# Chunk 1's first matrix product in a retention-plus-MLP kernel: seven block products for eight, and a new order table

## The chip, the cores and the metric

The kernel runs on one core of one Trainium2 chip. The metric is the device time of one execution in microseconds (us); smaller is better.

## What is computed

A retention layer (a linear attention with a decaying state, 4 batches, 8 heads, 768 steps, head size 64) feeds an MLP with a tanh-gelu:

```python
gamma = 1.0 - 2.0 ** (-5.0 - np.arange(H))
for t in range(S):                                   # S = 768
    state = gamma * state + k[:, :, t] (outer) v[:, :, t]
    y[:, :, t] = scale * q[:, :, t] @ state
x = y.transpose(0, 2, 1, 3).reshape(B * S, H * D)    # 3072 x 512
h = x @ w_in                                         # 512 x 2048
g = gelu_tanh(h)
out = g @ w_out                                      # 2048 x 512
```

## The kernel before

**Chunks.** The 768 steps are cut into six chunks of 128 steps; all four batches of a chunk make 512 tokens. For each chunk `att(c)` computes the retention output x (transposed, in fp16): it loads q, k and v, casts or scales them, transposes them on TensorE (`mm_T2`, L283, 64x64 matmuls against the identity), forms the scores (`mm_A`, L294), masks them on VectorE (L345), adds the part from the carried state (`mm_yc`, L313) and the part from the chunk itself (`mm_yi`, L325), and updates the state (`mm_s`, L336). Then M1 is h = x @ w_in with the gelu, and M2 is g @ w_out.

**Two forms of M1.** With plain blocks M1 takes 128 matmuls of 128x256 for a chunk. `m1_raw(c)` does that in 16 bank-fills of 8 matmuls each (`moe1_mm`, L426); each fill is read by one gelu on ScalarE (L442). `m1_w(c)` uses a Strassen-like scheme (`PROD`): both operands are seen as 2x2 blocks, and four groups `g` each do seven products of four matmuls (`m1w_mm`, L549), 112 in all. It pays with side work: sums of w_in blocks (`u_w`, made once on VectorE, L451), four sums of x blocks per chunk (`xs`, on GpSimd, L451; numbers 1 and 3 need all of x, 2 needs 1, 4 needs 2), and for each group three copies of a partial result from PSUM to SBUF (kind `snap`, L220, on ScalarE), three adds (kind `add`, L451, on VectorE) and four gelus, of which three read SBUF. Before the change chunk 0 uses `m1_first` (plain, as its x arrives batch by batch), chunk 1 uses `m1_raw`, and chunks 2 to 5 use `m1_w`. M2 of chunk 0 is plain (`m2_mm`, L572); M2 of chunks 1 to 5 has seven products (`m2w_mm`, L561) with sums of g (`s_g`, `sumg` on VectorE or GpSimd).

**What sets the order.** After a hand-written prologue every piece of work is an item with a kind, a list of what it needs and what it gives. `ORDER` is a table written out in the kernel: each word is an engine letter (p TensorE, a ScalarE, v VectorE, g GpSimd, s SyncE) and an item number, and the items are emitted in that order, so it fixes the order of every engine's queue, and by it which buffer an item takes (the slot that came free first). A word w puts idle matmuls on TensorE. `KIND` lists the engines on which a kind may run. An engine works through its queue in order: an instruction that waits holds up all behind it.

**Loads.** SyncE issues the loads of q, k and v as one chain of items in a fixed order (`load_in`, L791; for chunks 3 to 5 q comes as sixteen small transfers, `q_load`, L734), and the output stores (L582) stand between them where the table puts them. The chain begins behind a small copy on GpSimd (`hold`, L780), which waits for the third part of w_out. The loaded tiles are cast from fp32 to fp16 on GpSimd or VectorE (L222) or on ScalarE (L220), or scaled (L237).

**The in-place sum.** Sum number 3 of w_in (`sumw`, j = 3) overwrites a block of w_in itself, so it has to wait until the last plain reader is done. Before, that is `m1_raw` of chunk 1, group by group (`("m1raw", 1, i)`).

Of the kernel before, what the change touches and what calls it, by code (L numbers as in the profile page):

```python
# [18 lines left out]
s13 v137 v140 s14 s15 s16 s17 s18 a178 s19 g29 s20 s21 g26 v164 v156 v24 v157 v25 v141 s22
s23 p193 g35 s36 s37 p189 p187 a186 v153 v27 v147 v28 p207 a206 p209 p223 p225 a224 g32 s38  # L20
p211 p195 p197 p227 a194 a210 a196 p229 p199 p213 a222 p231 s39 a192 s40 a208 v149 s41 a226
a212 a198 p233 a232 p215 a214 a188 p217 p219 a216 v165 a230 a228 p201 a200 p203 p205 a202
a204 p806 p807 p808 p809 p810 p235 p811 p812 p221 p237 a236 p813 a218 a220 p814 p815 a816
p240 v238 v239 p246 v244 p818 a245 p243 p249 a234 v247 v241 v242 p262 p821 p824 v139 v248
v33 p825 p265 v158 a822 p267 v30 v31 v151 v34 a264 p826 a266 p827 p277 a276 a819 s42 s43 s44
s45 s46 p279 g58 g59 a828 s47 p252 a278 v155 s48 s823 a250 p258 v257 v251 p281 a256 p283
p285 a280 a282 a284 p261 v143 s829 v260 v259 p255 p263 v253 v254 p287 p289 a288 p271 a286
v150 p275 v167 v270 p269 a268 p273 p291 p293 p295 p297 v159 p299 v166 a49 a52 p301 a53 a50
v274 a292 a294 v272 a290 v310 v138 g55 g56 p338 a296 p326 a298 v308 v312 p344 a300 v146 s817
a336 a343 a337 s61 s820 s62 s63 v313 p303 a302 p305 p307 g51 s64 v309 g60 v324 v325 v316  # L30
a342 p347 p332 s65 a304 v54 a306 g320 p329 g57 g317 a331 g318 g321 v327 g322 v346 v345 v328
p830 p831 s66 a330 p335 v334 p341 v339 v340 v333 a832 p833 p834 v835 s67 p349 a74 p348 p357
p351 v350 p359 p361 v356 p355 g78 p353 v352 p836 p837 v154 p383 a384 p400 a401 p366 a367
v311 v358 v354 g362 g364 a70 a76 a72 p402 v314 g82 g363 p385 p839 s68 p840 s69 a838 v360
v403 v315 v386 a387 p368 v369 p373 g84 s86 s87 p388 p371 a372 a374 a389 a404 p417 p390 p842
v71 a418 a391 g365 g323 g77 g73 a370 p375 p843 s88 s89 v79 p405 p378 g80 v142 s90 v376 a377
p381 p395 p392 v319 v379 v83 a841 p419 v396 a380 p845 a406 a397 a382 g434 g435 g81 v420 v75
p407 p422 a408 a423 p409 g85 v162 v393 a394 v410 p424 a425 p412 v413 p426 v844 p398 p415
v427 a411 a416 p429 v430 a421 a399 p846 v847 s848 p452 v450 s91 p461 a414 a459 p432 a433
v460 p853 v451 v438 a431 g439 a428 g446 g447 g440 a99 g101 v442 g443 p467 p458 v465 p455  # L40
v453 v454 v456 g449 p849 v457 p850 a851 s852 s92 s93 v466 p854 p464 p469 v462 p468 p473 v463
p471 p479 a95 p481 a97 v470 v472 p477 v476 a107 p475 p856 v474 g482 p857 s94 g484 a103 v478
v480 v98 v96 p520 s111 a521 g436 p486 p488 g445 g105 g483 a855 v858 g102 p522 p503 a504 a487
a109 s112 s113 s114 s115 g106 g448 v489 g441 g485 g437 p859 v523 g110 p525 a526 p527 a528
p860 s116 s117 a490 p491 p532 p508 a524 p505 a509 v533 a534 p862 v506 v104 v108 a507 v444
p493 a494 p512 p510 v100 a511 a492 v513 a861 p537 p863 a864 p515 v516 a538 p495 v496 p498
a517 v499 a500 p529 p542 p539 v540 p865 a497 p501 a502 p544 p518 a545 v530 a519 p535 p866
p868 v554 a514 a120 v558 g559 v867 p869 v870 p549 a543 a541 a122 a536 g555 g557 a531 g562
v550 p872 a551 p546 p581 s871 s118 a579 v547 p572 v580 v570 a571 v556 p873 a874 v563 s875
p552 a553 a548 g566 p575 v574 v573 p584 g568 p587 p876 p877 p879 g567 p880 a878 g564 v585  # L50
p578 v582 v586 g560 v583 v577 v576 p589 p588 p591 p597 p595 g123 p601 v590 v596 v594 p599
p593 v592 g602 v600 g561 g603 v598 p882 p883 s119 a128 a132 a134 p885 a124 p606 a607 p640
p625 p623 a641 v881 g604 a884 a624 v626 p886 a887 p608 v609 p888 p889 p613 a614 v121 p630
a631 p628 a629 p642 a627 v569 v129 v133 p611 a612 p618 g135 v643 a644 p635 a610 p645 v636
a637 v619 p632 v633 a620 p615 p657 a634 g130 a658 v616 g126 a646 g565 p891 p647 g131 g605
p664 a665 p621 p638 a648 a622 a617 v890 g127 p649 v650 a651 a639 g678 p892 v893 s894 v676
p652 v653 p662 p669 p659 a663 v660 v670 p895 p896 p666 a661 a671 a654 v674 p655 g675 a656
p899 v667 a668 p672 a673 p701 a699 p692 v682 a897 v680 v691 v679 s898 g683 v686 v690 a700
p900 v687 g689 p902 p903 p707 p704 p695 g684 a901 v904 p905 p906 p908 a907 p909 v702 a910
g688 v125 v694 p911 v705 p698 v693 v706 v703 g681 g685 p709 p708 p912 v697 v696 p715 p717  # L60
p711 p713 v677 v710 v712 p914 p915 p773 a774 v716 v714 v916 s917 p722 g718 g720 p724 a723
v725 p756 a757 p739 a740 p729 a730 g719 p758 v759 a726 p775 v776 p744 p727 a760 a728 a745
p741 v742 p778 p746 g721 a777 a747 p734 v735 p761 p731 p763 v732 p748 v749 a743 p780 v913
a736 a764 p751 v752 p737 p754 p768 a779 a781 p785 a733 v786 a738 g790 g791 a762 v769 a755
a753 a750 a787 a770 g794 p918 p765 v766 g795 p782 v783 a767 p922 a784 p771 a772 p788 v798
a789 v802 p924 v803 p919 v805 a920 p926 v799 p928 a923 p930 s921 v927 v800 a925 p932 a933
p934 p936 a931 v793 v797 a935 a937 v804 v801 v792 v796 p938 v929 v939 p940 p943 p946 p949
v944 v941 s942 p952 a945 a950 v947 a951 a953 s948 s954
"""


# [1 line left out]
def kernel(  # L73
# [10 lines left out]
    B, H, S, Dh = q.shape  # L84
    C = 128
# [355 lines left out]
    def gelu(out, in_):  # L441
        nc.scalar.activation(out=out, in_=in_, func=AF.Gelu_apprx_tanh, scale=1.0)  # L442
# [357 lines left out]
    def att(c):  # L800
# [125 lines left out]
                S1(b)  # L926
        for par in range(2) if 0 < c < NCk - 1 else ():
            S(par)
        for j in (1, 3, 2, 4) if c > 1 else ():
            def emit(eng, j=j):  # L930
                xs[c] = T["xs", c]
                sum_of(eng, j, RHS, x_of4(c))

            need = {1: [("x", c, b) for b in range(B)], 3: [("x", c, b) for b in range(B)],
                    2: [("xs", c, 1)], 4: [("xs", c, 2)]}[j]
            op("sumx", emit, need + ([] if j == 1 else [("al", "xs", c)]), [("xs", c, j)],
               alloc=[(("xs", c), 1)] if j == 1 else [], early=[("al", "xs", c)] if j == 1 else [])
# [9 lines left out]
    def m1_first():  # L947
        for t0, t1, bs, cost, kind in ((0, half, (0, 1), 0.873, "gelu"), (half, half + C, (2,), 0.45, "gelu2"),
                                       (half + C, 2 * half, (3,), 0.45, "gelu2")):
            for fp in range(NP):  # L950
# [13 lines left out]
                   alloc=[(("g", 0, fp // 2), 1)] if new else [], early=[al] if new else [],  # L964
                   free=[key])
                last = [("m1done", 0)] if fp == NP - 1 and t1 == 2 * half else []
                pe(cost, emit, [("x", 0, b) for b in bs] + [("win" if fp else "winh", fp // 2)] + after("M1", t0), [key] + last,
                   [(key, 1, (128, 2, half))], [("x", 0)])

    def m1_raw(c):  # L970
        for t in range(2):
            for fp in range(NP):
                key = ("bank", "h", c, fp, t)

                def emit(fp=fp, t=t, key=key):
                    for r in range(2):
                        moe1_mm(c, 2 * fp + r, T[key][:, r], t * half, t * half + half)

                def ev(eng, fp=fp, t=t, key=key):
                    g_sb[c, fp // 2] = T["g", c, fp // 2]  # L980
                    gelu(g_tile(c, 2 * fp)[:, :, t * half:(t + 1) * half], T[key])

                new = fp % 2 == 0 and t == 0
                al = ("al", "g", c, fp // 2)
                op("gelu", ev, [key] + ([] if new else [al]),
                   [("H", c, fp, i, t) for i in range(2)],
                   alloc=[(("g", c, fp // 2), 1)] if new else [], early=[al] if new else [],
                   free=[key])
                last = fp == NP - 1 and t == 1
                pe(0.873, emit, [("x", c, 2 * t), ("x", c, 2 * t + 1)] + [("win", fp // 2)] + after("M1", c),  # L990
                   [key] + ([("m1raw", c, fp // 2)] if t and fp % 2 else []) + ([("m1done", c)] if last else []),
                   [(key, 1, (128, 2, half))], [("x", c)] if last else [])
# [322 lines left out]
```

## Time and profile before

| | |
|---|---|
| median of the runs shown | 196.97 us (196.82 to 198.26, 3 runs) |
| the profiled execution, own time | 199.29 us |
| its span, first to last instruction | 197.5 us |
| granted TensorE clock | 1.000 |
| busy: TensorE / VectorE / ScalarE / GpSimd | 189.3 / 142.1 / 123.0 / 104.6 us |
| matmuls | 2793 |
| L426 (plain M1 matmuls) | 320, 29.8 us busy |
| L549 (M1 matmuls in seven products) | 448 (rows xs,u_w; xs,w_in; x,w_in; x,u_w) |
| instruction DMAs (queues 8 and 14) | 22 and 7 packets, 0.42 MB |

A line number is that of the kernel before; a helper such as L451 (`tt`) or L220 (`copy_on`) serves many items, so its groups are told apart by the names of the tiles. Busy time of TensorE counts overlapping matmuls once. Idle time is put down to what released the engine. L549 before is chunks 2 to 5; the plain matmuls of chunk 1 are 128 of the 320 of L426.

### The profile page before, as it was taken

How to read it: one execution, taken by the hardware profiler on the slowest of the kernel's cores; microseconds unless marked ns; L12 is line 12 of the kernel's file. 1: busy time of each engine (PE TensorE's matmuls, PEld its weight loads, DVE VectorE, ACT ScalarE, POOL GpSimd, SP SyncE). 2: the span in 40 equal slices, each digit the busy share in tenths (PEclk: the TensorE clock that was granted, in tenths of full speed). 3: DMA queues.
4: the chain of work that ended last, by engine and by line, in shares of the span. 5: the costliest groups of instructions: out<-in, count | busy, mean ns of one | idle time of the engine just before them, and what ended most of it. 6: DMA issues, size and time to landing. Idle time of an engine off the chain costs nothing.

```text
span 197.5 us, 6582 instructions
## 1 busy us (share of the span) xinstructions
PE 189.3 (96%) x2793; PEld 154.2 (78%) x2793; DVE 142.1 (72%) x284; ACT 123.0 (62%) x237; POOL 104.6 (53%) x112
## 2 busy tenths in 40 slices
PE   7799999999999799999999999999999999999993
PEld 2357995556887688788888888888888888888882
DVE  4375042888599799779999885888867697675930
ACT  3367681143778611999948989629598810799321
POOL 2678000020107681997699995698953490818000
PEclk9999999999999999999999999999999999999999
DMA  6999999999989756998899879902002110200205
GB/s 151 287 261 205 207 206 196 247 238 204 205 214 231 207 91 137 238 208 135 157 257 240 153 132 226 311 32 53 3 0 110 47 63 3 106 0 3 108 3 212
DMA packets 96285, 30.06 MB, mean 152 GB/s; under 512 B 88320, under 2 KB 93184, under 8 KB 96256
## 3 DMA queue, kind: packets, MB, share of 16 engines
q1 hardware_dynamic: 84976, 23.35, 50.4%
q0 software_dynamic: 4752, 4.19, 13.2%
q10 hardware_dynamic: 6528, 2.10, 4.2%
q8 instruction: 22, 0.36, 0.7%
q14 instruction: 7, 0.06, 0.1%
HBM read 27.54 MB, written 6.29 MB: 171 GB/s over the span
## 4 chain that ended last, share of the span: by engine, by line
PE 80%; DMA 7%; SPq 6%; ACT 2%; issue 1%; POOL 1%; ACTq 1%; DVE 0%
PE ps L561 28%; PE ps L549 24%; PE ps L426 13%; PE ps L572 7%; SPq L734 6%; DMA w_in<-in_moe_w_in_dram 3%; DMA st<-in_k_dram 3%; PE ps L294 3%; PE ps L325 2%; PE ps L283 2%; DMA ldq<-in_q_dram 1%; PE ps L336 1%; PE ps L313 1%; ACT qk L220 1%; POOL qk L237 1%
## 5 line engine op out<-in xcount | busy, mean ns | idle before, releaser
L451 DVE TENSOR_TENSOR st<-ps,st 128x512 f32<-128x512 f32 x48 | 31.5, 683 | 12.2 <-ACT st L220 6.4
L442 ACT ACTIVATE g<-ps 128x512 f16<-128x512 f32 (+1 forms) x56 | 28.6, 547 | 16.0 <-PE ps L426 14.9
L561 PEld LDWEIGHTS <-s_g 128*128 128x128 f16 x320 | 30.8, 98 | 4.2 <-issue 0.2
L345 DVE TENSOR_TENSOR a<-ps,mask 128x512 f16<-128x512 f32 x44 | 27.4, 682 | 6.7 <-PE ps L294 6.5
L220 ACT COPY st<-ps 128x512 f32<-128x512 f32 x48 | 26.3, 598 | 8.6 <-PE ps L549 8.5
L442 ACT ACTIVATE g<-st 128x512 f16<-128x512 f32 x48 | 29.1, 644 | 1.7 <-DVE st L451 1.5
L426 PE MATMUL ps<-x,w_in 128*128 128x256 f16 (+1 forms) x320 | 29.8, 252 | 0.3 <-DMA w_in<-in_moe_w_in_dram 0.3
L426 PEld LDWEIGHTS <-w_in 128*128 128x128 f16 x320 | 25.5, 98 | 3.6 <-DMA w_in<-in_moe_w_in_dram 0.5
L451 POOL TENSOR_TENSOR s_g<-g 128x512 f16<-128x512 f16 x18 | 21.3, 1192 | 12.5 <-ACT g L442 12.5
L549 PEld LDWEIGHTS <-w_in 128*128 128x128 f16 x256 | 24.9, 98 | 3.2 <-ACT st L220 0.3
L220 ACT COPY o<-ps 128x512 f32<-128x512 f32 (+1 forms) x28 | 14.3, 532 | 19.9 <-PE ps L561 15.9
L561 PEld LDWEIGHTS <-g 128*128 128x128 f16 x240 | 22.9, 98 | 3.1
L549 PEld LDWEIGHTS <-u_w 128*128 128x128 f16 x192 | 18.7, 98 | 2.9 <-DVE st L451 0.7
L561 PE MATMUL ps<-w_out,s_g 128*128 128x256 f16 x160 | 19.6, 273 | 0.0
L561 PE MATMUL ps<-w_out,g 128*128 128x256 f16 x160 | 19.3, 273 | 0.0
L220 ACT CAST qk<-ldq 64x512 f16<-64x512 f32 (+1 forms) x19 | 11.5, 623 | 12.6 <-DMA ldq<-in_q_dram 7.5
L561 PE MATMUL ps<-t_w,s_g 128*128 128x256 f16 x160 | 19.1, 273 | 0.0
L451 POOL TENSOR_TENSOR s_g<-s_g,g 128x512 f16<-128x512 f16 x13 | 15.1, 1168 | 6.4 <-DVE s_g L451 6.1
L549 PE MATMUL ps<-xs,u_w 128*128 128x256 f16 x128 | 17.8, 273 | 0.5 <-DVE st L451 0.5
L549 PE MATMUL ps<-xs,w_in 128*128 128x256 f16 x128 | 17.6, 273 | 0.0
L549 PE MATMUL ps<-x,w_in 128*128 128x256 f16 x128 | 16.6, 273 | 0.0
L237 POOL TENSOR_TENSOR v<-ld,cst 128x512 f16<-128x512 f32 x14 | 14.8, 1069 | 1.8 <-DMA ld<-in_v_dram 1.8
(74 smaller groups left out, 277.7 us busy)
## 6 DMA issues: line engine op xcount, KB each, us to landing
ld<-in_v_dram SPq DMA_DIRECT2D x19, 256.0 KB, 4.4
ld<-in_k_dram SPq DMA_DIRECT2D x17, 256.0 KB, 5.0
out_dram<-o SPq DMA_DIRECT2D x8, 512.0 KB, 3.4
ldq<-in_q_dram SPq DMA_DIRECT2D x48, 64.0 KB, 2.6
w_out<-in_moe_w_out_dram POOLq DMA_DIRECT2D x4, 512.0 KB, 14.2
w_in<-in_moe_w_in_dram POOLq DMA_DIRECT2D x3, 512.0 KB, 7.7
ld<-in_q_dram SPq DMA_DIRECT2D x5, 256.0 KB, 5.8
out_dram<-o SPq DMA_DIRECT2D x5, 256.0 KB, 4.3
```

The lines of the kernel that those rows point to most:

```text
L220: eng.copy(out=out, in_=in_)
L237: eng.tensor_tensor(out=o, in0=heads(src, sw), in1=heads(cst[:, col:col + H].unsqueeze(2), sw).broadcast_to([128, NHP, 2, Dh]), op=ALU.mult,)
L283: nc.tensor.transpose(out=ps[m][j * 64:(j + 1) * 64, n + i, hp], in_=h16[nm, c, b][rows, 2 * hp + j], identity=iden[rows, rows],)
L294: nc.tensor.matmul(out=ps[j][m * 64:(m + 1) * 64, hp], lhsT=t[j * 64:(j + 1) * 64, 1, hp, m * 64:(m + 1) * 64], rhs=t[j * 64:(j + 1) * 64, ...
L345: eng.tensor_tensor(out=a_sb[c, b, j], in0=ps, in1=mask[:, j], op=ALU.mult)
L426: nc.tensor.matmul(out=out, lhsT=w_in_sb[wi][:, kc, wr * 128:(wr + 1) * 128], rhs=xT[c][:, kc, t0:t1], start=(kc == 0), stop=(kc == NHP - ...
L442: nc.scalar.activation(out=out, in_=in_, func=AF.Gelu_apprx_tanh, scale=1.0)
L451: eng.tensor_tensor(out=out, in0=in0, in1=in1, op=op)
L549: nc.tensor.matmul(out=ps[:, f], lhsT=m1_lhs(lk, kc, 2 * g + f), rhs=x[:, kc], start=(n in FIRST and kc == 0 and f == 0), stop=(n in (1, 5 ...
L561: nc.tensor.matmul(out=ps, lhsT=m2_lhs(c, lk, fp, a), rhs=m2_rhs(rk, fp), start=(first and fp == 0), stop=(n in (1, 5, 6) and fp == NP - 1 ...
L572: nc.tensor.matmul(out=ps, lhsT=g_sb[0, fc // 4][:, fc % 4, b * C:(b + 1) * C], rhs=w_out_sb[fc // 4][:, fc % 4], start=(fc == 0), stop=(f ...
L734: eng.dma_start(out=t[p0:p0 + 32, :, a, :], in_=src[j, dd, t0:t0 + 32])
```

## The change

`m1_raw` is removed and chunk 1 goes through `m1_w` as the later chunks do. For that the xs sums are made for chunk 1 too, and the in-place sum of w_in waits for chunk 0's plain M1 instead (a new token `("m1part", 0, fp, t0)` that every bank-fill of `m1_first` gives). The table `ORDER` is a new one from its second word on, for all engines; its comment in the change is that its rows pause at instruction fetches.

```diff
 ORDER = """
-p169 a168 v9 v10 g8 p179 p181 w1 p174 v180 g0 p172 g11 p191 g1 g2 g3 a173 p177 v170 v171
-a190 g4 g5 g6 v175 v176 v144 v160 v161 v145 v136 v152 p185 a184 v163 v148 p183 a182 g7 s12
...
+p169 v9 v10 a168 a8 g0 g1 g2 g3 p181 g4 g5 g6 p179 w1 p174 a173 p172 v170 a180 p191 a190
+p177 v171 g11 g7 s12 s13 p185 a178 v176 s14 s15 s16 g26 v175 s17 g29 s18 s19 s20 s21 v140
...
 """
...
-        for j in (1, 3, 2, 4) if c > 1 else ():
+        for j in (1, 3, 2, 4) if c else ():
             def emit(eng, j=j):
                 xs[c] = T["xs", c]
                 sum_of(eng, j, RHS, x_of4(c))
...
-                pe(cost, emit, [("x", 0, b) for b in bs] + [("win" if fp else "winh", fp // 2)] + after("M1", t0), [key] + last,
+                pe(cost, emit, [("x", 0, b) for b in bs] + [("win" if fp else "winh", fp // 2)] + after("M1", t0),
+                   [key, ("m1part", 0, fp, t0)] + last,
                    [(key, 1, (128, 2, half))], [("x", 0)])
-
-    def m1_raw(c):
...
             op("sumw", ew, [("win", i)] + {2: [("sw", 1, i)], 4: [("sw", 2, i)],
-               3: [("sw", 1, i), ("m1raw", 1, i)]}.get(j, []), [("sw", j, i)])
+               3: [("sw", 1, i)] + [("m1part", 0, 2 * i + r, t) for r in range(2) for t in (0, half, half + C)]}.get(j, []), [("sw", j, i)])
...
         att(c)
-        (m1_raw if c == 1 else m1_w)(c)
+        m1_w(c)
         g_sums(c)
```

More of the change, by code (lines that the diff above doesn't have):

```diff
@@ L16 @@
 ORDER = """
-p169 a168 v9 v10 g8 p179 p181 w1 p174 v180 g0 p172 g11 p191 g1 g2 g3 a173 p177 v170 v171
-a190 g4 g5 g6 v175 v176 v144 v160 v161 v145 v136 v152 p185 a184 v163 v148 p183 a182 g7 s12
[L19 to L68, printed above, removed]
+p169 v9 v10 a168 a8 g0 g1 g2 g3 p181 g4 g5 g6 p179 w1 p174 a173 p172 v170 a180 p191 a190
+p177 v171 g11 g7 s12 s13 p185 a178 v176 s14 s15 s16 g26 v175 s17 g29 s18 s19 s20 s21 v140
@@ new lines @@
+s22 g32 s23 v160 v161 g35 v163 v144 v145 v136 v141 v148 v149 p183 a182 v150 v137 v156 v157
+p193 a192 p189 p187 p207 a186 p209 a208 v158 v152 v153 p223 a206 p225 p227 v138 a224 p229
+v155 p195 a194 p197 a222 a228 p211 p213 a196 p231 p233 a226 a212 a210 v146 p199 p201 p215
+p203 a198 a214 a202 a200 p846 v147 p217 a216 p219 p221 a218 v164 v24 a184 p847 p235 a230
+a232 v25 a188 a234 p205 a204 p848 p849 v139 a220 p850 p851 p852 v165 p853 p237 v162 s36 s37
+v27 v28 p240 s38 s39 s40 a238 a239 p854 p855 a856 p243 v242 v241 p246 a245 a244 p858 a859
@@ new lines @@
+v154 p861 g49 p249 p262 p265 p864 p865 a264 v30 v247 v248 v142 p267 v31 a236 a862 s41 p252
+v166 v33 v34 a266 a250 s42 a251 s43 s44 s45 v143 s46 p866 p331 a332 p258 v151 a256 p255 p333
+p316 v257 p261 v253 v254 p314 a315 v260 v259 v334 g50 v317 p867 a868 p263 p269 v268 p271
+a270 p275 v274 a318 g276 g278 p297 p280 a298 a281 g55 g277 g56 s47 s48 s863 s857 g279 p299
+v300 p282 v283 a335 a301 g52 g53 p273 p304 v272 a305 p287 a288 g58 g59 s61 s62 s63 s869 p338
+g51 s64 p285 p302 v167 a339 a286 p292 a303 a284 g54 p309 v293 a294 s65 v310 a311 p289 p306
@@ new lines @@
+p378 v290 a291 v376 v377 v307 p336 a337 p343 v344 p295 a296 p319 a320 v348 p321 a322 p366
+v364 p372 v365 a371 v370 a308 p323 v324 p312 a313 g352 p369 v367 p384 a382 a383 p326 v327
+a328 g353 g57 a345 p340 v341 a342 v368 p329 a330 p375 v373 g60 p381 v380 v374 p870 p346 a347
+g360 g361 g354 v379 p871 a325 s66 a872 p387 v385 v386 p388 p389 p391 s860 v390 p395 p393
+v392 p399 v394 p401 p397 v396 g402 g404 p873 p442 s67 v400 p440 a441 p406 a407 p874 v443
+v875 g349 g403 a444 p408 v409 p413 p423 p425 a414 a424 p411 v398 v426 v356 g357 v159 p457
@@ new lines @@
+a412 a410 p428 p418 v419 a458 a429 p430 a431 v359 g70 a78 p415 a72 a82 p459 v460 a461 p432
+p447 p435 v436 g74 a76 a427 s68 s69 s86 v416 a80 a448 a437 p876 p877 p445 a446 p879 p880
+g362 g405 g350 g84 s87 p464 a465 a420 p452 p462 p421 v363 g77 v79 a878 p449 a463 v83 v433
+a422 g81 v355 v358 p438 a434 a417 v450 v453 p469 v470 p882 p455 p883 g476 a881 p466 a451
+v351 a454 v474 v71 a439 v75 s88 a456 p885 g482 v478 g483 v467 p501 v499 p492 a500 v490 v491
+g73 g85 p886 v887 a468 g475 s888 a471 p472 a473 v884 g480 s89 g95 s90 s91 s92 p893 p495 v493
@@ new lines @@
+g479 g486 p507 g97 v506 p504 v503 v502 v494 p889 p890 a891 s892 p894 g487 s93 p498 p509 p508
+v505 p515 p511 v496 v497 p517 p521 p519 a103 a895 p513 v510 v512 a99 v514 a107 v96 p896 p897
+p543 a544 v516 g522 p562 g524 p526 a527 p560 v520 v898 g105 g523 g101 g485 g102 s94 s111
+a561 v518 v484 p899 p545 p900 s112 s113 g477 g525 g98 a901 p528 v529 v104 a530 p550 p548
+a551 a549 s114 g110 v563 v546 a547 a564 v489 p565 p531 p902 g481 p555 p533 v556 a534 a532
+v488 p567 p903 p538 a557 a109 a566 a568 v539 a540 p535 g106 v536 a537 v100 p552 v553 p905
@@ new lines @@
+p577 p541 a904 p906 a554 a542 a578 p584 p558 p569 p572 v108 v907 p582 v570 v573 a571 v596
+a559 v594 v598 v595 s115 v599 a585 p579 v580 p908 p909 v910 s911 a583 g601 a574 s116 p575
+a120 a576 g602 g603 p589 g600 g122 p586 v587 v590 p612 a581 a591 v611 p621 a588 a610 v620
+p912 p913 p592 a593 v606 v607 p916 p917 a914 a619 g604 p618 s117 s118 p615 v613 v614 p624
+g123 v623 a918 v617 s119 p919 p920 p922 v921 p923 g608 s915 a924 v622 p627 v616 p629 p628
+p631 v625 v626 p633 v630 p639 p635 v634 v632 v638 p641 v597 p637 v636 g609 a132 g124 p925
@@ new lines @@
+p926 p680 p663 a664 a927 g128 g642 g644 v129 g643 p665 v666 p646 v605 a647 p648 v649 a650
+v640 v133 a681 g645 p928 p929 p682 p653 v683 a654 p931 p697 a698 a126 p651 a652 p668 a669
+a667 p932 v131 v933 p658 v659 g135 a684 p704 a660 p655 p670 v656 a705 v930 a671 p672 p702
+v121 a703 v673 a657 p685 p661 a662 p675 p687 a688 v714 v676 v715 a674 g127 p706 s934 v707
+a686 p678 a677 a679 g130 g134 g718 g719 p699 v700 p935 a701 p709 v710 a708 p689 a711 v690
+a691 p936 a937 s938 p692 v693 a694 p939 p695 p712 a696 a713 v722 g716 p741 v740 v724 p732
@@ new lines @@
+a730 a739 p940 a941 p942 p943 v726 v727 v723 p945 p946 g725 g720 g729 v717 p747 a731 p735
+v125 p738 a947 v728 v944 g721 v746 v733 v734 v736 p948 p949 a950 v745 p951 p952 v737 p748
+v953 p744 p749 v742 p954 v743 p751 p753 v750 v752 p757 v756 p755 v754 g758 p955 v956 s957
+g760 p796 a797 p762 a763 p779 a780 p764 v765 g759 p798 p813 v799 p815 p786 a814 v816 a800
+p781 a766 v782 a787 p784 a785 p818 a819 p767 a768 p801 p788 a817 p791 v792 a783 v789 g761
+p769 a770 p820 a821 p771 v772 p822 p774 p803 p777 v775 v823 a790 a793 a802 p794 a804 a795
@@ L69 @@
+a776 v834 g835 a773 a824 a778 p825 v826 a827 p805 v806 p808 v809 a810 g832 p962 p958 v836
+p811 p828 a829 v842 a812 v830 v831 a807 v838 v843 v839 g841 a963 p959 a960 s961 p964 p966
+p968 g844 g837 v840 p970 a965 p972 v845 v833 v969 v967 a971 a973 p974 a975 p976 a977 p978
+v979 p980 p983 v984 v981 s982 a985 p986 p989 v987 s988 p992 a990 a991 a993 s994
 """
@@ L966, in m1_first @@
                 last = [("m1done", 0)] if fp == NP - 1 and t1 == 2 * half else []
-                pe(cost, emit, [("x", 0, b) for b in bs] + [("win" if fp else "winh", fp // 2)] + after("M1", t0), [key] + last,
+                pe(cost, emit, [("x", 0, b) for b in bs] + [("win" if fp else "winh", fp // 2)] + after("M1", t0),
+                   [key, ("m1part", 0, fp, t0)] + last,
                    [(key, 1, (128, 2, half))], [("x", 0)])
-    def m1_raw(c):
[L971 to L992, printed above, removed]
     def m1_w(c):
```

## The prediction

> **What bounds the kernel now.** I read the page's head first, then the chain that ended last, then TensorE's timeline around every place where its records leave a hole, then the waits of the engine that stood before such a hole.
>
> ```profile
> span 197.5 us, 6582 instructions
> PE 189.3 (96%) x2793; PEld 154.2 (78%) x2793; DVE 142.1 (72%) x284; ACT 123.0 (62%) x237; POOL 104.6 (53%) x112
> PE   7799999999999799999999999999999999999993
> PEclk9999999999999999999999999999999999999999
> ...
> 168.18 10.48 PE ps L549 x96
> ```
>
> The PE row is full in nearly every slice and the granted clock is full in all, so after the prologue (the first product of M1 starts at 15.38) the end is set by the sum of what TensorE issues, plus the holes. The last line, from the chain, gives the price of one 128x256 matmul in a run: 10.48 / 96 = 0.109 us. The other engines have room on average, so they matter only where TensorE waits for them. There are few such places, all between 61 and 85 us:
>
> ```profile
> 56.40 5.41 PE L426 MATMUL ps<-x,w_in 128*128 128x256 f16 x48
> 61.82 0.32 PE L283 MATMUL ps<-iden,qk 64*64 64x64 f16 x16
> 62.57 0.90 PE L283 MATMUL ps<-iden,qk 64*64 64x64 f16 x80 [0.43 <-POOL qk L222]
> 63.40 2.79 PE L426 MATMUL ps<-x,w_in 128*128 128x256 f16 x24
> 66.12 0.42 PE L294 MATMUL ps<-qkT 64*64 64x128 f16 x16
> 66.37 0.35 PE L283 MATMUL ps<-iden,qk 64*64 64x64 f16 x22
> 67.90 0.28 PE L283 MATMUL ps<-iden,qk 64*64 64x64 f16 x10 [1.18 <-issue]
> 67.99 0.42 PE L294 MATMUL ps<-qkT 64*64 64x128 f16 x16
> 68.34 1.92 PE L561 MATMUL ps<-w_out,g 128*128 128x256 f16 x16
> ...
> 80.40 0.60 PE L549 MATMUL ps<-x,w_in 128*128 128x256 f16 x4
> 81.46 1.49 PE L549 MATMUL ps<-xs,u_w 128*128 128x256 f16 x12 [0.46 <-DVE st L451]
> ```
>
> In this view of TensorE (start, length, line, count, hole before it and who ended it) the holes, counted from start to start, are: P1, 0.6 at 62.0, transposes of chunk 2 (L283) that wait for casts on GpSimd; P2, 1.4 at 66.5, in the middle of transposes with nothing to wait for that the profile shows ("issue"); P3, 81.46 - 80.40 - 4 x 0.109 = 0.6 at 80.8; and two small ones behind it that I get in the same way, P4, 0.3 together. Sum 2.9 us. P3 has a history, in the chain and in ScalarE's timeline:
>
> ```profile
> 75.75 2.56 DMA ldq<-in_q_dram
> 78.33 0.62 ACT qk L220
> ...
> 79.60 1.08 ACT st L220 x2
> 80.71 0.70 DVE st L451
> 81.46 2.36 PE ps L549 x20
> ```
> ```profile
> 78.33 1.25 ACT L220 CAST qk<-ldq 64x512 f16<-64x512 f32 x2 [7.45 <-DMA ldq<-in_q_dram]
> ```
>
> ScalarE stood 7.45 us in its queue at a cast of chunk 3's q, which the sixteen q transfers (L734) fed only at 78.31; the three PSUM copies that M1 of chunk 2 needed were queued behind it, the vector add behind those, and TensorE behind the add.
>
> **The change, part by part.** *Matmuls.* In chunk 1, 16 bank-fills of 8 matmuls become 4 groups of 7 products of 4: 128 become 112. The instruction lists of the two programs agree: 2793 against 2777. 16 x 0.109 = -1.75 us, on TensorE's own time, with nothing over it.
>
> *Tile shapes.* The new order goes from 128x128 matmuls to the small ones of the attention and back 31 times, against 28 before. Going in: 24 matmuls from 63.40 to 66.12 are 2.72 us where 24 x 0.109 is 2.62, so 0.10. Coming back: 16 of L294 took 0.35 before L561 (67.99 to 68.34) and 0.25 before L283 (66.12 to 66.37), so 0.10. Three excursions are 0.6; three more changes from one small shape to another, whose starts lie 0.045 apart in the trace where those in a run lie 0.003 to 0.03 apart, make it about +0.7. Net of work: -1.05 us.
>
> *Side work.* Chunk 1 gains 12 PSUM copies (L220, 0.598 each), 12 vector adds (L451, 0.683), 12 gelus that read SBUF (0.644) in place of PSUM (0.547 to 0.6), and 4 xs sums on GpSimd (L451, 1.154). The lists also show 8 casts moved to GpSimd, five of them from ScalarE and three from VectorE. ScalarE: 12 x 0.598 + 12 x 0.05 - 5 x 0.6 = +4.8 us; VectorE: 12 x 0.683 + two s_g sums x 0.48 - 3 x 0.41 = +7.9; GpSimd: 4 x 1.154 - 2 x 1.19 + 8 x 0.695 = +7.8. From 46 to 70 us, where it goes, the windows show ScalarE busy for 11.58 of 16 and 5.25 of 8, so 7.2 idle; VectorE 13.35 and 6.66, so 4.0 idle, with 3.8 more from 33 to 46 (9.23 of 13), where its sums of w_in and w_out can stand; GpSimd 9.5 of 24. I cost it at nothing on the path, because TensorE has chunk 2's transposes and chunk 0's M2 to put between the products. Without that cover it is rival C.
>
> *P1 and what takes its place.* GpSimd's queue in the changed program has, in a row: cast of chunk 2's q of batch 2, third xs sum of chunk 1, cast of its k, fourth xs sum, then the casts of batches 1 and 3. So the third xs sum, and with it M1 of chunk 1, now stands behind a cast that waits for a load. Adding up the changed list of TensorE from 18.69 (where the old chain is in the middle of M1 of chunk 0) up to the first product with the third sum: 48 + 60 matmuls x 0.109, 128 short ones x 0.056, 64 of L572 x 0.216, and 6 us for chunk 1's attention with its excursions, comes to 57.6. The loads can't come earlier: SP's order up to the last v of chunk 2 is the old one, and it starts behind the same gate (the weights that land at 32.6). The load in question was issued at 49.82 and its kind takes 5.8 us (median), so 55.6; cast 0.6, sum 1.15: 57.4. That is a margin of 0.2 where a single SP issue ran 1.5 us longer than its neighbours (2.64 at 51.02). So 0 to 1.4 us of a new wait; I take the middle, 0.7. The chunk 2 transposes come behind it and then have over 1 us to spare, so P1 goes: -0.6 + 0.7.
>
> *P2.* The same stretch of dense small matmuls (transposes, scores, transposes) is in the new order, at nearly the same time. 0 to 1.5; I take 1.2: -0.2. The Trainium skill ("Runtime: NRT & Kernel Launch", Instruction fetch mechanics) says that instructions come in blocks of 256 by the sequencer's own DMA queue and that crossing a block is mostly hidden. The profile's queue 8 agrees with the blocks (22 packets, 0.36 MB); if P2 is such a crossing it was not hidden, and by the rule's word "hidden" the new sum would be 1.2 lower.
>
> *P3.* In ScalarE's new queue, 8 copies and 2 gelus of M1 of chunk 2 stand ahead of the first cast of chunk 3's q, and SP has two output stores ahead of the q transfers instead of three (0.4 to 0.8 each). The cast is reached at about 78 to 79, as the load lands. 0 to 0.6; I take 0: -0.6. *P4* is of a size that any order has: I leave it, 0 to 0.5.
>
> Sum: -1.05 - 0.6 + 0.7 - 0.2 - 0.6 = -1.75 us against a span of 197.5. The profiled execution took 199.29, 1.8 over its span; the median of the runs shown is 196.97. I take the difference off the median: about **195.3**, own range 195.0 to 196.3.
>
> **Rivals.** *A, the holes close (faster by more than 1%).* Loads in time and no P2: -1.05 - 2.9 + 0.3 = -3.65, so 193.3; with P2 alone left, 194.5. I put it at 194.2. For it: every hole of before has a cause that the new queues move. Against: the margin of 0.2 above, and P2's dense stretch is still there. The skill's rule on fetches would land here.
>
> *B, the holes only move.* The waits add up to 2.9 again, elsewhere; only the work is saved: 196.97 - 1.05 = 195.9, and up to 197.0 if they grow by one. For it: TensorE gets to chunk 2's transposes 3 us sooner (about 58.7 against 61.82), the loads don't, and the DMA share was 1.00 and 0.93 in the windows from 33 to 62.
>
> *C, ScalarE becomes the pace of M1 of chunk 1 (slower).* One group of seven products is 28 x 0.109 = 3.06 us of TensorE, but 3 x 0.598 + 3 x 0.644 + 0.6 = 4.3 us of ScalarE, as the rows have them. Over four groups TensorE would wait 5.1 us if nothing else filled it: -1.05 + 5.1 = +4, so 201. It decides once more than 3 us of it is uncovered. Against: 7.2 us idle on ScalarE in that stretch against 4.8 added, and between these products stand chunk 2's transposes and scores, the last of chunk 1's attention and pieces of chunk 0's M2. That the change doesn't do what it says is out: the lists show the 112 matmuls.
>
> **Chances.** Forecast 0.39, A 0.36, B 0.14, C 0.11. What a measurement of this kernel can tell from no change is about 1%, 2 us: faster by more is A, 0.36; within it are the forecast and B, 0.53; slower is C, 0.11. The range goes from the middle of A to the far side of B, 193.6 to 197.7, and leaves out C and A's best.
>
> **What would show it.** Right: 2777 matmuls, no hole near 80 us, one of 1 to 1.5 "issue" in transposes near 65, one under 1 before an xs, w_in product of chunk 1, released by GpSimd near 58. Wrong: ScalarE ahead of holes from 47 to 66 (C), holes over 3 us in sum (B), or none over 0.5 (A).

## The result, and the profile after

The changed kernel takes 195.88 us (median of 18 runs, 195.01 to 197.37), the kernel before in the same comparison 197.42 (18 runs, 196.32 to 200.29). The ratio is 0.9934, 95% interval 0.9911 to 0.9957: 1.5 us less, a real gain and smaller than 1%. The forecast was 195.3 with an own range of 195.0 to 196.3.

The head of the page, after. The first line is the span, the second the busy time of each engine, the last TensorE in 40 slices:

```profile
span 194.7 us, 6611 instructions
PE 187.6 (96%) x2777; PEld 152.7 (78%) x2777; DVE 152.0 (78%) x295; ACT 125.3 (64%) x244; POOL 112.3 (58%) x122
PE   7787999999999999999999999999999999999993
```

2777 matmuls, as the lists said. The slice with a 7 near 65 us is gone; a new 7 stands at 15 to 20 us. TensorE's timeline (start, length, line, count, hole before it and who ended it) says what is there now. The helper lines of before are two higher here: L283 is L285, L549 is L551.

```profile
18.25 1.05 PE L428 MATMUL ps<-x,w_in 128*128 128x256 f16 x8 [1.02 <-DMA w_in<-in_moe_w_in_dram]
...
57.54 1.04 PE L551 MATMUL ps<-x,u_w 128*128 128x256 f16 x8
58.41 1.04 PE L551 MATMUL ps<-xs,w_in 128*128 128x256 f16 x8
...
65.73 0.90 PE L296 MATMUL ps<-qkT 64*64 64x128 f16 x32
66.56 1.05 PE L563 MATMUL ps<-w_out,g 128*128 128x256 f16 x8
...
79.91 0.60 PE L551 MATMUL ps<-x,u_w 128*128 128x256 f16 x4
80.35 1.91 PE L563 MATMUL ps<-t_w,s_g 128*128 128x256 f16 x16
```

- Near 58, where I expected a wait of 0.7 for the third xs sum: none. 57.54 + 8 x 0.109 = 58.41.
- Near 66, where I expected "issue" of 1.0 to 1.5: a hole of 0.23 inside the 32 scores (it starts at 65.87; it is too short for the timeline to split the row).
- Near 80: nothing.
- At 17.0: a hole of 1.08 that I had not forecast. The first M1 product on the second half of w_in's first part waits for that half, which landed at 18.21; before, it landed at 16.69 and TensorE asked for it at 17.17.

**A ledger for every profile.** One profile of each kernel is a thin basis: the lists of times spread over 2 to 4 us. So I cut each profile into the same pieces, from TensorE's matmul starts: the start of the first M1 product, the holes (what an interval between two starts has over the median of its pair of shapes in all profiles, where that is more than 0.09), the work (all the rest of the time up to the last start, so smaller delays count as work), and the 3.4 behind the last start. With the kernels of the experiments, told below:

| profile | M1 starts | work | holes | where (us: size) |
|---|---|---|---|---|
| before | 15.38 | 175.49 | 3.25 | 61.9: 0.62, 66.5: 1.37, 80.7: 0.62, rest small |
| before, again (b_again) | 15.70 | 175.42 | 0.28 | 65.9: 0.28 |
| b_hold | 15.73 | 175.42 | 0.79 | 65.9: 0.79 |
| b_split | 16.81 | 175.34 | 0.62 | 41.6: 0.38, rest small |
| b_less | 15.54 | 173.71 | 4.88 | 49.7: 0.57, 61 to 62: 1.25, 66.3: 1.03, 80.0: 1.29, rest small |
| b_less_hold | 16.66 | 173.68 | 1.66 | 65.3: 1.18, 98.1: 0.40 |
| after | 15.38 | 174.52 | 1.45 | 17.0: 1.08, 65.9: 0.23 |
| after, again (a_again) | 15.52 | 174.49 | 0.79 | 57.4: 0.65 |
| a_split | 16.71 | 174.50 | 0.13 | |
| a_xs | 15.46 | 174.50 | 1.86 | 69.1: 0.62, 74.6: 0.60, rest small |
| a_both | 15.27 | 174.66 | 0.59 | 18.1: 0.46 |
| a_xs_hold | 15.46 | 174.50 | 0.14 | |
| a_more | 15.44 | 176.35 | 0.13 | |
| a_exc | 15.57 | 180.58 | 0.39 | |

The work column repeats to 0.15 and is 0.9 less after than before. The holes do not repeat. Of P1, P2 and P3, which I took from one profile of before, a second profile of the same kernel has only P2, at 0.28. From the spans of all timed runs the typical idle time follows: median span less work, less 15.38, less 3.4; a later start of M1 counts as idle time here. For before it is 195.6 - 175.4 - 18.8 = 1.4 us, for after 194.1 - 174.5 - 18.8 = 0.8. So the gain of 1.5 is about 0.9 of work and 0.6 of idle time. Which holes make up that 0.6 in a typical execution, two profiles of each kernel do not show.

### The profile page after: what moved, and what is told of

Same layout as the page of the kernel before. It is cut to its first block, busy times and chain, and to the rows that moved or that the text cites. A ratio compares the mean times of both kernels' runs of the same rounds, so it can differ in the third digit from the quotient of the medians.

```text
span 194.7 us, 6611 instructions
## 1 busy us (share of the span) xinstructions
PE 187.6 (96%) x2777; PEld 152.7 (78%) x2777; DVE 152.0 (78%) x295; ACT 125.3 (64%) x244; POOL 112.3 (58%) x122
## 4 chain that ended last, share of the span: by engine, by line
PE 89%; DMA 7%; POOL 1%; ACTq 1%; ACT 0%; issue 0%
PE ps L563 32%; PE ps L551 32%; PE ps L574 7%; PE ps L428 7%; DMA w_in<-in_moe_w_in_dram 4%; PE ps L296 3%; DMA st<-in_k_dram 3%; PE ps L327 3%; PE ps L285 2%; PE ps L315 1%; PE ps L338 1%; ACTq L162 1%; POOL qk L239 1%; POOL w_in L409 0%; ACT o L222 0%
## 5 line engine op out<-in xcount | busy, mean ns | idle before, releaser
L453 DVE TENSOR_TENSOR st<-ps,st 128x512 f32<-128x512 f32 x60 | 39.0, 679 | 5.9 <-PE ps L551 4.1
L222 ACT COPY st<-ps 128x512 f32<-128x512 f32 x60 | 32.5, 592 | 14.5 <-PE ps L551 14.3
L444 ACT ACTIVATE g<-st 128x512 f16<-128x512 f32 x60 | 36.0, 643 | 4.6 <-DVE st L453 4.5
L551 PEld LDWEIGHTS <-w_in 128*128 128x128 f16 x320 | 30.9, 98 | 4.1
L444 ACT ACTIVATE g<-ps 128x512 f16<-128x512 f32 (+1 forms) x44 | 21.6, 528 | 7.5 <-PE ps L428 7.0
L551 PEld LDWEIGHTS <-u_w 128*128 128x128 f16 x240 | 23.2, 98 | 2.8
L551 PE MATMUL ps<-xs,w_in 128*128 128x256 f16 x160 | 22.1, 273 | 0.0
L551 PE MATMUL ps<-xs,u_w 128*128 128x256 f16 x160 | 21.6, 273 | 0.0
L551 PE MATMUL ps<-x,w_in 128*128 128x256 f16 x160 | 20.8, 273 | 0.0
L453 POOL TENSOR_TENSOR xs<-x 128x512 f16<-128x512 f16 x10 | 11.7, 1174 | 11.3 <-DVE x L354 9.7
L453 POOL TENSOR_TENSOR s_g<-g,s_g 128x512 f16<-128x512 f16 x10 | 11.9, 1199 | 9.0 <-DVE s_g L453 5.7
L428 PE MATMUL ps<-x,w_in 128*128 128x128 f16 (+1 forms) x192 | 15.1, 237 | 1.3 <-DMA w_in<-in_moe_w_in_dram 1.3
```

The source lines that it names most:

```text
L222: eng.copy(out=out, in_=in_)
L428: nc.tensor.matmul(out=out, lhsT=w_in_sb[wi][:, kc, wr * 128:(wr + 1) * 128], rhs=xT[c][:, kc, t0:t1], start=(kc == 0), stop=(kc == NHP - ...
L453: eng.tensor_tensor(out=out, in0=in0, in1=in1, op=op)
L551: nc.tensor.matmul(out=ps[:, f], lhsT=m1_lhs(lk, kc, 2 * g + f), rhs=x[:, kc], start=(n in FIRST and kc == 0 and f == 0), stop=(n in (1, 5 ...
```

## The experiments

Ratios are to the kernel before, run beside each. The changed kernel, run once more beside the first two, gave 195.87 (12 runs), 0.9923 [0.9898, 0.9947].

**1. Each kernel a second time** (no edit).

> The kernel before once more, one look. The profiled execution took 199.29, the lowest of the times shown 196.32: so 3 us of holes that come and go. If P1, P2 and P3 are of every execution, they are again 0.6, 1.4 and 0.6 (span 197.5); if they come and go with the transfers, at least one is under 0.3 and the span is 195 to 196.5.

> The changed kernel once more, for a second execution with a profile and for times beside the others of this call. If the 17.0 hole is a chance of timing (fetch packet against the last piece of the weights), it may be absent or of another size, 0 to 1.1; if it comes from the order of the triggers it is again 0.9 to 1.2. No hole at 58 (third xs sum), none over 0.4 at 80. Time 195.9 +- 0.5.

b_again: 197.07, span 194.8; P1 and P3 absent, P2 0.28. They come and go. a_again: no hole at 17, but the wait that the prediction named, at 57.4. The chain of waits of a_again around it (start, length, what):

```profile
50.56 5.56 DMA ld<-in_q_dram
...
56.24 0.61 POOL qk L224
...
56.92 1.16 POOL xs L453
...
58.12 1.03 PE ps L551 x8
```

Load 5.56, cast 0.61, sum 1.16, and TensorE, whose product before it (from 56.60, 8 x 0.109) was through at 57.47, waited until 58.12. In the first profile the same load landed at 54.70, not 56.12, but that is not why there is no hole in it. GpSimd's timeline there, cast and sum:

```profile
56.31 0.61 POOL L224 CAST qk<-ld 128x512 f16<-128x512 f32 x1
56.88 1.15 POOL L453 TENSOR_TENSOR xs<-x 128x512 f16<-128x512 f16 x1
```

The cast stood behind the second xs sum and not behind the load, and the third sum ran at the same time as in a_again, to 58.03. TensorE got there 0.9 later, at 58.41, because it had lost 1.08 at 17.0. So one hole covered another, and the price of the queue order stayed hidden.

**2. What P2 is: before and after with 84 instructions more on TensorE ahead of the work.** The new helper `spin4` makes 56 idle matmuls of 128x128 in place of 14 of 128x512.

```diff
-    spin(14)
+    spin4(14)
```

> The kernel before, with the fourteen idle 128x512 matmuls of the prologue cut into 56 of 128x128: the same columns, 84 more instructions (weight loads and matmuls) on TensorE, none of them in the timed work. Theory (instruction fetch): in before the hole P2 sat at TensorE's instruction 1981, in after a hole of 0.24 at its instruction 1982, 256 x 7 + 190 in both, though the work there differs; it ended 2.30 and 2.36 us after a 16 KB instruction packet started. So it is tied to the place in the instruction list. With 84 more ahead, the boundaries fall on old instructions 1641, 1897 and 2153; by the starts in the trace of before those blocks last 5.25 us or more against the 5.25 that the slowest packet and its latency take, so no hole over 0.3 at 66 us, the profile's span 1.0 to 1.4 shorter there, and the median 0.4 to 1.3 below before. Rival (TensorE waits at that point for data or a queue): the hole of 1.0 to 1.4 stays in the same transposes near 66.5, and the time is that of before within 0.3.

> The changed kernel with the same cut of the prologue's fourteen idle matmuls. Theory (instruction fetch): the hole of 1.08 at 17.0 us, the wait for the second half of the first part of w_in, comes from a 16 KB instruction packet that started at 16.2 on the DMA engine that had the last piece of that half (its 4-byte packet started at 17.16, the other fifteen by 16.31). With 84 more instructions the block ends earlier and the packet starts before 13: hole under 0.3 there. The hole at instruction 1982 (65.9) goes from its place; the new boundary is in scores near 64.0, 0 to 0.6. Time 0.3 to 1.2 below the changed kernel. Rival (the earlier triggers of the weights' later parts slow that half): the hole at 17.0 stays at 0.9 to 1.2, time within 0.3 of the changed kernel.

b_split: 197.87 (12 runs), 1.0023 [0.9998, 1.0048]. a_split: 196.33 (12 runs), 0.9967 [0.9933, 1.0]. The place of P2 came out as the theory has it: it is gone in both. By itself that proves little, as a_again has no hole there without any edit; the table further down is the proof. TensorE's timeline of b_split, the same stretch that held "[1.18 <-issue]" before:

```profile
67.16 0.42 PE L301 MATMUL ps<-qkT 64*64 64x128 f16 x16
67.41 0.42 PE L290 MATMUL ps<-iden,qk 64*64 64x64 f16 x32
67.66 0.40 PE L301 MATMUL ps<-qkT 64*64 64x128 f16 x16
```

The 32 transposes (L290 here) run through. But the time I expected did not come, because M1 starts late:

```profile
14.78 0.42 PE L301 MATMUL ps<-qkT 64*64 64x128 f16 x16
16.81 0.94 PE L433 MATMUL ps<-x,w_in 128*128 128x256 f16 x7 [1.61 <-DMA w_in<-in_moe_w_in_dram]
```

TensorE's first instruction packet (16 KB, 0.95 us, one packet on one DMA queue) now started at 12.65 and not at 15.8. The w_in transfer that M1 waits for comes in halves, and each half lands in sixteen parts, each with a packet of 4 bytes at its end. The trace has the times (us):

| profile, half of w_in | instruction packet starts | fifteenth part lands | sixteenth part lands |
|---|---|---|---|
| before, first | 15.80 | 15.18 | 15.33 |
| before, second | 15.80 | 16.54 | 16.69 |
| b_split, first | 12.65 | 15.16 | 16.76 |
| a_split, first | 12.57 | 15.12 | 16.67 |
| after, second | 16.20 | 16.67 | 18.21 |
| a_again, second | 16.69 | 16.59 | 16.84 |

Everywhere else, in all fourteen profiles, the sixteenth part follows the fifteenth by less than 0.5 us, in both halves. Where the packet started at 12.6 it is 1.6 behind (in the second half too, 18.17 and 18.05), and in after, where the packet came at 16.20, 1.5. So the packet held up one part of sixteen, and that is also the 17.0 hole in after. In a_again the packet came when that half had been read, and there is no hole.

My rival, the earlier triggers of the weights, falls: a_again has them too. The trace does not name a packet's DMA engine; that the late part is that of the engine with the packet is inferred. A packet can fall into a transfer without harm: those of before and of a_both (15.80 and 16.16) did. Why the part is late by 1.5 to 1.6 when the packet took 0.95 is not shown. What I missed in the expectation is that moving the packet ahead of the second half put it ahead of the first as well.

The Trainium skill ("DMA: Bandwidth & Descriptors", Queues, rings and completion order) says that a DMA engine's semaphore increment lands only after all its earlier writes, across its queues. The trace of after agrees with that: the last 4-byte packet of the half started at 17.16, as the instruction packet ended, and its part landed 1.05 later; for the other parts that step took about 0.4.

The places where TensorE stood still at "issue", in all kernels. The index counts the weight loads and matmuls ahead of the hole (counted so, it is 1982 in both kernels), the packet is the last of TensorE's instruction queue ahead of it:

| profile | index, work there | packet starts | hole ends | difference | hole |
|---|---|---|---|---|---|
| before | 1982, transposes | 65.60 | 67.90 | 2.30 | 1.37 |
| b_again | 1982, transposes | 63.81 | 66.19 | 2.38 | 0.28 |
| b_hold | 1982, transposes | 64.24 | 66.73 | 2.49 | 0.79 |
| b_less | 1982, scores | 64.91 | 67.33 | 2.42 | 1.03 |
| b_less_hold | 1982, scores | 64.12 | 66.50 | 2.38 | 1.18 |
| after | 1982, scores | 63.74 | 66.11 | 2.37 | 0.23 |
| a_both | 446 = 1982 - 6 x 256, state sums | 16.16 | 18.57 | 2.41 | 0.46 |

The index stays while the work under it changes. b_less shows it in TensorE's timeline: with 32 instructions fewer ahead, the "issue" left the transposes and stands in the scores behind them:

```profile
65.99 0.42 PE L283 MATMUL ps<-iden,qk 64*64 64x64 f16 x32
66.24 0.28 PE L294 MATMUL ps<-qkT 64*64 64x128 f16 x6
67.33 0.35 PE L294 MATMUL ps<-qkT 64*64 64x128 f16 x10 [0.81 <-issue]
```

So P2 is a crossing into a block of 256 instructions whose packet started less than about 2.4 us before. The fourteen profiles have 288 crossings for which the packet can be found. These seven are the only ones with a hole at the boundary (over 0.09, as in the ledger), and in none did it pass sooner than 2.30 us after the packet's start; the nearest passes without a stop came at 2.44 to 2.56 (a_split, b_again, a_more, a_xs). The packet starts after TensorE has entered the block ahead, in before 1.0 to 2.9 us later up to 69 us and under 2.0 from 73 us on. So a short block is the one at risk: the block of transposes and scores that ends here lasts 3.8 us in before and 3.7 in after, all others in these two profiles 4.2 to 14. In after the packet started 1.6 after TensorE entered that block, in before 2.9; that 1.3 covers the difference of 1.1 between the holes. Why it starts sooner I have not settled; in after SyncE has two output stores ahead of the q transfers in that stretch and before has three, and the DMA share from 62 to 70 us is 0.69 and not 0.85, but no run isolates it.

**3. The price of the work, in the old order: 16 matmuls left out.** One of the eight matmuls of each bank-fill of chunk 1.

```diff
-        for kc in range(NHP):
+        for kc in range(NHP - (c == 1 and fc % 2)):
...
-                stop=(kc == NHP - 1),
+                stop=(kc == NHP - 1 - (c == 1 and fc % 2)),
```

> The kernel before with one of the eight matmuls of each of the sixteen bank-fills of chunk 1 left out (the last quarter of the contraction for the odd columns): 16 matmuls fewer, the number that the change saves, with the old order and no side work. Theory (TensorE sets the end, so its own time comes off in full): 16 x 0.109 = 1.75 below before, 1.4 to 2.1. Rival (the holes behind take part of it back, since loads and casts come no sooner): 0.5 to 1.2 below, with the holes P1 or P3 longer by as much in the profile.

197.19 (10 runs), 0.9978 [0.9950, 1.0007]. The work fell by 1.72 in the ledger, 0.1075 for a matmul, as costed; the time by 0.2. The theory is out; the time moved as the rival has it, but even less than the 0.5 that it gave. TensorE's waits in its profile (an execution of 199.23; before's profile was one of 199.29, so the two compare):

```profile
PE ps L549 <- DVE st L451: 1.1, 1, 1.1
PE ps L283 <- POOL qk L222: 1.0, 2, 0.6
PE ps L294 <- issue: 0.8, 1, 0.8
```

These are P3, P1 and P2. P1 grew by 0.63 and P3 by 0.67 against the profile of before, 1.3 of the 1.72 saved. TensorE came sooner, the casts and copies behind the loads did not. That is one long execution of each kernel. For those near the median, whose idle time is 2.9 us against 1.4 in before by the reckoning above, no profile of this kernel shows the holes, and that they are the same is only argued; b_less_hold in experiment 8 speaks against it.

**4. The price of the work, in the new order: 16 matmuls put back.**

```diff
+        again = (2 if n == 0 else 1) if c == 1 and n in FIRST else 0
         for f in range(2):
-            for kc in range(2):
+            for kc in [0] * (again if f == 0 else 0) + [0, 1]:
```

> The changed kernel with 16 matmuls of chunk 1 done twice (the first one of each product that opens a bank, for one of them in each group three times): the 16 that the change saves are put back, with the new order and all the side work. Theory (in the new order TensorE itself sets the pace in that stretch, so its work counts there in full): 195.87 + 16 x 0.109 = 197.6, 197.2 to 198.0. Rival (as in the old order, where taking 16 out was worth only 0.2: the loads set the pace up to chunk 2, and the work before them is nearly free): 195.9 to 196.6.

197.19 (12 runs), 1.0002 [0.9984, 1.0021]: 1.3 above the changed kernel, the low end of what the theory gave, and far from the rival. Here most of it counts. The profile has next to no holes (0.13 in the ledger); its span is 195.3, and TensorE is busy for all but 5.3 of it:

```profile
PE 190.0 (97%) x2793; PEld 154.7 (79%) x2793; DVE 151.8 (78%) x295; ACT 125.9 (64%) x244; POOL 113.0 (58%) x122
```

This kernel has the matmul count of before, the new order and the side work, and takes the time of before. So the new order by itself gains nothing: its work is 0.9 more than that of before, for the most part by the extra tile shapes, and its idle time is 0.4 in place of 1.4. The saved matmuls by themselves gained 0.2 in the old order. It is the two together that make 1.5 us.

**5. The price of an excursion to a small tile.** One idle 128x64 matmul ahead of 24 products.

```diff
+        if c > 3 and n in FIRST:
+            nc.tensor.matmul(
+                out=ps[0:64, 0, 0:64], lhsT=zero[:, 0:64], rhs=zero[:, 0:64], start=True, stop=True, skip_group_check=True
+            )
```

> The changed kernel with one idle 128x64 matmul put in front of each of the 24 products of chunks 4 and 5 that open a bank (L551): 24 more excursions from 128x128 matmuls to a small shape and back, nothing else. Theory (my term of 0.10 in and 0.10 back): 24 x (0.20 + 0.02 for the matmul itself) = 5.3 us more span, 4.5 to 6.0. Rival (the shape changes are hidden, only the small matmul counts): 24 x 0.02 to 0.05 = 0.5 to 1.2.

201.82 (4 runs), 1.0234 [1.0183, 1.0284], 5.9 above the changed kernel. The work rose by 180.58 - 174.50 = 6.08, 0.253 for each, some 0.02 of it the matmul itself (16 such in a run, at 13.87, begin within 0.25). The theory holds, at its upper end.

**6. The wait for the third xs sum.** Two words swapped on GpSimd.

```diff
-... g55 g277 g56 ...
+... g277 g55 g56 ...
```

> The changed kernel with two words of the order swapped on GpSimd: the third xs sum of chunk 1 ahead of the cast of chunk 2's q of batch 2, which waits for a load. Theory (P1's replacement is that wait): in the changed kernel's second profile TensorE waited 0.65 us at 57.4 for that sum, with the load landing at 56.12, and in its first profile, with the load landing at 54.70, not at all. With the swap the sum can start when x is there, near 55.4, and TensorE finds it done in every execution: no hole at 57 to 58, median 0.1 to 0.5 below the changed kernel's 195.9. Rival (the wait moves on to chunk 2's transposes, whose casts now come 1.2 us later): a hole of 0.3 to 1.2 in L285 near 59 to 61, median 195.9 or above.

195.32 (7 runs), 0.9894 [0.9859, 0.9929], 0.55 below the changed kernel's median; the intervals overlap, so the size is open. The profiled execution was its longest, 197.06, with late loads, and shows the swap at work. GpSimd's timeline:

```profile
55.77 1.16 POOL L453 TENSOR_TENSOR xs<-x 128x512 f16<-128x512 f16 x1
57.50 0.61 POOL L224 CAST qk<-ld 128x512 f16<-128x512 f32 x1 [0.57 <-DMA ld<-in_q_dram]
58.33 0.61 POOL L224 CAST qk<-ld 128x512 f16<-128x512 f32 x1 [0.23 <-DMA ld<-in_k_dram]
```

The sum was done at 56.93; behind the cast it would have ended at 59.2. No hole over 0.1 at 57 to 61, so the rival did not show in this execution. TensorE waited further on, at 69.1 for a scaling of v and at 74.6 for an xs sum, both on GpSimd, 0.6 each; GpSimd itself had stood 1.40 us at a load of v that came at 65.2.

**7. The swap, and the block boundary moved from behind the first packet.** The idle matmul `w1` replaced by 36 small ones, which adds 70 instructions behind the first boundary.

```diff
-... p179 w1 p174 ...
+... p179 w36 p174 ...
...
-... g55 g277 g56 ...
+... g277 g55 g56 ...
```

> The same swap, and the one idle 128x512 matmul of the prologue (word w1) replaced by 36 idle 128x64 ones: 70 more instructions on TensorE, behind the first boundary (instruction 190, crossed at 13.2 us) and in a stretch where TensorE waits anyway. Theory (instruction fetch): the first packet stays near 16, away from the first half of w_in, so M1 starts at 15.3 to 15.7 and not at 16.7 as in the two kernels with the cut idle matmuls; the boundary of 65.9 us moves 70 instructions up, where its block lasts longer: no hole over 0.6 at 64 to 66. Median 0 to 0.4 below the kernel with the swap alone. Rival (the 36 matmuls cost more than the wait covers): M1 starts later than 15.7, median 0.2 to 0.8 above the kernel with the swap alone.

195.74 (10 runs), 0.9933 [0.9904, 0.9962]: no gain on the swap alone. M1 starts at 15.27 and nothing stands still at 64 to 66, as the theory has it. But I had not costed the block in between, which now passes through short matmuls too: it lasts 5.0 us, and its packet started 3.1 after TensorE entered it. TensorE's timeline:

```profile
18.05 0.25 PE L338 MATMUL ps<-v,qk 128*64 128x64 f16 x3
18.57 0.26 PE L338 MATMUL ps<-v,qk 128*64 128x64 f16 x5 [0.27 <-issue]
```

It is the seventh row of the table in experiment 2: the rule held, my use of it did not.

**8. The load chain started sooner.** The gate on the second part of w_out, in three kernels.

```diff
-            eng.tensor_copy(out=T["lq", "q", 1, 0][0:1, 0, 0:1], in_=w_out_sb[2][0:1, 0, 0:1])
+            eng.tensor_copy(out=T["lq", "q", 1, 0][0:1, 0, 0:1], in_=w_out_sb[1][0:1, 0, 0:1])
-        op("hold", emit, [("wout", 2)], ["held"])
+        op("hold", emit, [("wout", 1)], ["held"])
```

> The kernel before with the gate of the load chain (hold) on the second part of w_out in place of the third: the chain starts at 30.4 and not at 32.9. Theory (the loads of chunks 2 and 3 are what P1 and P3 wait for): loads land 1 to 2.5 sooner, P1 (62) and P3 (80) under 0.2, median 0.4 to 1.2 below before's 197.4. Rival (the transfers share a full pipe until 62, so the weights come later by what the loads come sooner): a wait for w_out of 0.5 to 2.5 near 34 to 42 and no gain, 197.4 to 199.

> The kernel before with the earlier gate and with the sixteen matmuls of chunk 1 left out (the last quarter of the contraction for the odd columns). Theory (without the wait for the loads the saved matmuls count): 1.3 to 1.8 below the kernel with the earlier gate alone, where without that gate they were worth 0.2. Rival (something else behind them takes the time back): 0 to 0.6 below it.

> The changed kernel with the third xs sum ahead of the cast and the earlier gate. Theory (late loads are what is left in the slower executions): median 0.2 to 0.7 below the 195.3 of the kernel with the swap alone, and a smaller spread (highest under 196.5). Rival (weights late instead): a wait for w_out near 34 to 42 of 0.5 or more, 195.5 to 197.

b_hold 197.22 (12 runs), 0.9996 [0.9974, 1.0019]; b_less_hold 196.91 (12 runs), 0.9971 [0.9941, 1.0001]; a_xs_hold 195.29 (6 runs), 0.9907 [0.9885, 0.9928]. No effect in any of the three, for a reason that neither theory had. SyncE's queue in b_hold:

```profile
30.70 0.37 SPq L791 DMA_DIRECT2D ldq<-in_q_dram  x1
...
32.15 3.17 SPq L791 DMA_DIRECT2D ldq<-in_q_dram  x1
...
36.26 1.94 SPq L791 DMA_DIRECT2D ld<-in_v_dram  x2
```

The first issue is 2.2 us sooner than before (30.70 against 32.89), the third takes 3.17 us in place of 1.25, and the fifth starts at 36.26 where before it started at 36.12. Of chunk 2's loads, the one that P1's replacement hangs on was issued at 49.21, against 49.82 and 49.70 in the two profiles of before. The loads were hardly sooner, so this tells nearly nothing of what late loads cost. In particular the 0.3 that b_less_hold gained on b_hold does not test whether the sixteen matmuls would count with early loads. b_less_hold's profile, close to its median, has none of P1 and P3 and yet 1.66 of holes and an M1 that starts at 16.66. The late start comes from one scaling on VectorE, which stood ahead of the masks that TensorE waited for. It took 2.37 us, where the same one took 0.68 in b_hold:

```profile
10.46 2.37 DVE L237 TENSOR_TENSOR qk<-ld,cst 128x512 f16<-128x512 f32 x1
```

The largest hole is P2, 1.18 against 0.79 in b_hold: with 32 instructions fewer the block ahead of the boundary lasts 3.6 us and not 3.9, while the packet started at 64.12 and 64.24. So part of the saved work can be lost at the instruction packet, too. By the reckoning above the median of b_less_hold has 2.7 us of idle time; how often which of these makes it up is open.

## Why the prediction was right, and where its steps were not

The median of 195.88 lies in the forecast's own range. The term for the work was right; that the terms for the holes added up was in part luck. The forecast was a drop of 1.75 from 196.97, the median of three runs; with 18 runs that median is 197.42, and the drop is 1.5.

- *Matmuls, -1.75:* -1.72 in the ledger of b_less. Right in size. "On TensorE's own time, with nothing over it" was wrong as a general statement: in the old order 0.2 of it reaches the end, in the new one 1.3 (experiments 3 and 4).
- *Tile shapes, +0.7:* the net of work came out at -0.9 where I had -1.05, so the shapes cost 0.8. An excursion measured alone is 0.25. Right.
- *Side work, nothing:* right. No hole from 46 to 70 us names ScalarE or VectorE, and rival C is out. It was close for VectorE. The window after (the stretch and its length; busy us of PE, PEld, DVE, ACT, POOL; granted clock, DMA share, GB/s):

```profile
46.00:62.00 16.00, 16.00 (x299) 12.01 (x297) 15.84 (x33) 12.93 (x26) 10.42 (x14) 1.00 1.02 233
```

  VectorE is busy for 15.84 of 16 us and TensorE still does not wait. Over the page VectorE gained 9.9 us (I had 7.9), ScalarE 2.3 (4.8) and GpSimd 7.7 (7.8).
- *P1, -0.6, and its replacement, +0.7:* the mechanism was right and seen, 0.65 at 57.4 in a_again, by the load, cast and sum that the step lists. It is not in every execution, as its range of 0 to 1.4 had it. The step's own list adds up to 57.5 and not 57.6, so the margin against the load was 0.1 and not 0.2.
- *P2, stays at 1.2:* the step that failed. It was 0.23, and there is no hole at that place in a_again and in all later variants of the new order. I argued from "the same stretch of dense small matmuls". What counts is the time from the start of the instruction packet to the crossing, of which about 2.4 us are needed, and in after the packet came 1.3 us sooner than in before, counted from TensorE's entry into the block ahead. The rule of the Trainium skill that I cited ("Runtime: NRT & Kernel Launch", Instruction fetch mechanics) has the block size right, and "mostly hidden" too: one crossing of 22 in before was not.
- *P3, -0.6:* it is gone, and the ScalarE queue is as I had it (the first cast of chunk 3's q begins at 79.11, behind the copies, without a wait). But it was not there in b_again, b_hold or b_split either, so the median had less of it to give.
- *The sum against the profiled execution:* 199.29 was 1.9 above before's median. I took its 2.9 us of holes as the kernel's; the typical idle time is 1.4. Holes taken off one long execution were too dear, and the 1.2 that I left for P2 made up for it: that is the luck. The 1.08 at 17.0 was in no term.
- *Rivals:* B's figure (195.9) is the measured one, and its mechanism (only the work is saved) is nearer to the ledger than a sum of single holes: 0.9 of work, 0.6 of idle time. A took all holes as closed and came to 193.3 to 194.5. With next to no holes (a_xs_hold, 0.14) the kernel takes 195.20, and the lowest of all runs of the change is 195.01: A subtracted holes that a typical execution of before does not have.

## What to carry to other kernels

A hole in one profile is one draw: before it is put into a sum, profile the kernel a second time and compare the profiled execution's time with the median. Split the span into work and holes; the work term transfers, and whether it reaches the end depends on the order around it: taking the work out alone, and putting it back alone, shows it. What holds it back in the old order, loads, casts or instruction packets, is not settled here. Of the versions run here those with the third xs sum ahead of the cast have the lowest times (0.9894 and 0.9907, and 0.9933 with the 36 small matmuls, against 0.9934 and 0.9923 for the change), but the intervals overlap.

## What was not expected of the hardware

- An instruction packet can cost time twice. TensorE passed into a new block of 256 instructions no sooner than 2.3 us after the packet's start in any of 288 crossings, and stood still where it came sooner: seven times, at a fixed instruction index whatever the work, six of them at the end of a block of 3.6 to 3.9 us. And a packet of 0.95 us that falls into a transfer split over sixteen parts can make the last part land 1.5 to 1.6 us behind the others; on which DMA engine it ran, the trace does not say.
- Starting a chain of loads 2.2 us sooner, while the weights fill the DMA engines, gained nothing: the third issue then took 3.17 us in place of 1.25, and the chain was back on its old times at the fifth.
